# The order of the two column pieces in FFN's second product

## The chip, the cores and the metric

The kernel runs on one core of one Trainium2 chip. The metric is device time in microseconds (us): the median of several executions. One further execution is recorded by the hardware profiler, and every line of a profile or a trace below is from that one. Its engines are called PE (TensorE's matmuls), PEld (TensorE's weight loads), DVE (VectorE), ACT (ScalarE), POOL (GpSimd) and SP (SyncE).

## What is computed

A layer norm of x feeds two branches. One is attention over eight positions at a distance of two, with 32 heads of 20 columns; the other is a feed-forward network (FFN). Their product is added to x.

```python
def reference(A_x, A_wqkv, A_wo, B_w1, B_w2):      # 2048 tokens, D = 640, F = 1536
    xn = _layernorm(A_x)
    s = attention(xn, A_wqkv) @ A_wo               # 8 keys per token, 2 apart; 32 heads of 20
    h = _silu(xn @ B_w1)                           # 2048 x 1536
    g = _silu(h @ B_w2)                            # 2048 x 640: FFN's second product
    return A_x + s * g
```

## The kernel before

**Precision.** Each matrix product is made of three products. Both operands are split into a high and a low half (`th` and `tl` for the normed x and later for the attention's output, `sh` and `sl` for FFN's hidden values, and both halves of a weight block side by side in a ring of seven `w` buffers). High by high, high by low and low by high are added up in one bank of PSUM.

**Groups and stages.** The 2048 tokens are worked through in four groups of 512, each four tiles (t = 0 to 3) of 128. For each group the stages on TensorE are: the products for q, k and v (lines 737 to 739; the first quarter of the first group at line 676), from the second group on the output projection of the group before (`wo_phase`), and FFN (`ffn_phase`). The last group's projection (`wo_last`) ends the kernel.

**FFN.** F is cut into 12 blocks of 128, taken two at a time. `up(f)` makes a block of hidden values with 15 matmuls of 512 columns (lines 882 to 884) in a bank called `rot`. ScalarE's silu writes it out as `sh` (line 888) and as `sf` (line 889), and VectorE subtracts the two to get `sl` (line 890). `down((f, f + 1))`, the second product, adds both blocks' share to the output: 128 tokens by 640 columns for each of the four tiles. It first runs through both blocks' high halves, for each tile the pair of pieces with the weights' high half and then the pair with the low half; after that through both blocks' low halves, one pair a tile. That is 24 pairs of matmuls, called a run here. Six runs a group make 24 in all.

**The two pieces.** 640 columns don't fit one bank (512), so `tm_mm` issues each product as two matmuls with the same stationary tile `st`: a wide piece of CA = 384 columns (line 766) into the tile's own bank `a[t]`, and a narrow piece of CB = 256 (line 768) into one half of a bank `b[t // 2]` that two tiles share. Each matmul has a weight load (LDWEIGHTS) of its own in the instruction stream, so a pair loads the same tile twice. `wo_phase` and `wo_last` use `tm_mm` as well.

**The banks.** Six banks called `acc` go round by count (`bank()`). FFN takes all six. At the end of a group's FFN, ScalarE's silu (line 936) empties them into `gate`, the four wide banks first and then the two narrow ones; in the last group the order is wide, narrow, three wide, narrow. The next stage's products for q, k and v take the same banks in the same order, so its first matmul (line 737) writes the bank that ScalarE emptied first.

**What sets the order.** All work is entered in a list with durations and priorities, and a planner (class `Weave`) orders each engine's instructions by simulating them; TensorE's own work stays in the order in which it is entered. A whole call of `big` or `small` in `down` is one entry of TensorE, with the banks of both pieces as what it writes. The waits on semaphores are worked out afterwards from the buffers that each instruction touches.

Of the kernel before, what the change touches and what calls it, by code (L numbers as in the profile page):

```python
# [18 lines left out]
DC, FC = D // P, F // P  # L19
# [34 lines left out]
def tsl(t):  # L54
    return slice(t * P, (t + 1) * P)
# [157 lines left out]
def local_attention_silu_ffn(ctx: ExitStack, tc: tile.TileContext, x, wqkv, wo, w1, w2, out):  # L213
# [64 lines left out]
    def rot():  # L278
        i = take("rot", 2)
        return ROT[i], ("rot", i)  # L280
# [7 lines left out]
    def dve(n, fn, reads, writes, prio, lock=False):  # L288
        add("DVE", dv(n), fn, reads, writes, prio, lock)

    def act(n, fn, reads, writes, prio, table=None):
        add("ACT", ac(n), fn, reads, writes, prio, table=table)

    def pe(dur, fn, reads, writes):
        add("PE", dur, fn, reads, writes)
        clock[0] += dur
# [128 lines left out]
    def w_next(*want):  # L425

        i = used[0]
        assert units[i] == want and i < loaded[0], (units[i], want)
        used[0] += 1
        s, n = i % RING, width(want)  # L430
        return WR[s][:, :n], WR[s][:, n:2 * n], ("wh", s), ("wl", s)

    def w_done(n=1):
        for _ in range(n):
            w_load()


    def load_x(g, t, n=1, prio=None):
        dma(lambda: nc.sync.dma_start(XIN[:, t:t + n], rows(xg, g)[:, t:t + n]), [],
            [("xin", u) for u in range(t, t + n)], n * P * D * 4, clock[0] if prio is None else prio,  # L440
            late=LATE if g else 0.4 * t)

    def ln_stats(t, after=()):
        st = ST[t % 2]
        ks = ("st", t % 2)
        for k in range(2):
            dve(320, lambda k=k: nc.vector.bn_stats(out=st[:, k, :], in_=XIN[:, t, k * 320:(k + 1) * 320]),
                [("xin", t), *after], [ks + (k,)], 1)
        dve(60, lambda: nc.vector.bn_aggr(out=MV[:, t, :], in_=st), [ks + (0,), ks + (1,)], [("mv", t)], 1)

    def ln_rstd(a, b, at=1, after=()):
        n = range(a, b)
        act(b - a, lambda: nc.scalar.activation(SD[:, 0, a:b], MV[:, a:b, 1], AF.Sqrt, bias=epst, scale=1.0),
            [("mv", t) for t in n] + list(after), [("sd", t) for t in n], 0, "sqrt")
        dve(10, lambda: nc.vector.reciprocal(out=SD[:, 1, a:b], in_=SD[:, 0, a:b]),
            [("sd", t) for t in n], [("rs", t) for t in n], at)
# [53 lines left out]
    def turn_o(cs, s, ks, i, both=False):  # L510

        for k, c in enumerate(cs):
            qs = range(c * P // CQ, ((c + 1) * P - 1) // CQ + 1)
            dve(TOK, lambda k=k, c=c: nc.vector.transpose(  # L514
                out=s[:, k, :TOK].rearrange("p (j t b) -> p t j b", j=NB, t=T),
                in_=O[:, :, c * P:(c + 1) * P].rearrange("p t (j a) -> p t j a", j=NB)),
                [("o", q, t) for q in qs for t in (0, 2)], [ks[k]], 2)
        move(s, ks, cs, "ot", ["turned"], both)
        for c in cs:
            split_sb(c, moved("ot", c), i, 0 if both else 0.4)  # L520
# [233 lines left out]
    def t_keys(i, cs, ts=range(T), kinds=("th", "tl")):  # L754
        return [(k, i, c, t) for k in kinds for c in cs for t in ts]

    def tm_banks(narrow_first=False):
        b = [bank() for t in range(T // 2)] if narrow_first else None
        a = [bank() for t in range(T)]
        return a, b or [bank() for t in range(T // 2)]  # L760

    def tm_mm(banks, t, st, w, first, last, cols=(0, 1)):
        a, b = banks
        h = t % 2
        if 0 in cols:
            nc.tensor.matmul(a[t][0][:, :CA], st, w[:, :CA], start=first, stop=last)  # L766
        if 1 in cols:
            nc.tensor.matmul(b[t // 2][0][:, h * CB:(h + 1) * CB], st, w[:, CA:], start=first and h == 0,  # L768
                             stop=last, skip_group_check=True)

    def tm_views(banks, order="aaaabb"):

        a, b = banks
        n = {"a": 0, "b": 0}
        for kind in order:
            k = n[kind]
            n[kind] += 1
            if kind == "a":
                yield a[k][0][:, :CA].rearrange("p (t m) -> p t m", t=1), a[k][1], slice(k, k + 1), slice(0, CA)
            else:  # L780
                yield b[k][0].rearrange("p (t m) -> p t m", t=2), b[k][1], slice(2 * k, 2 * k + 2), slice(CA, D)

    def gkeys(ts, cs):
        return [("g", t, cs.start) for t in range(ts.start, ts.stop)]
# [84 lines left out]
    def ffn_phase(g, i, ix, io):  # L869
        nxt = g + 1 if g + 1 < NG else None  # L870
        ps = tm_banks()
        a, b = ps

        def up(f):
            wh, wl, kh, kl = w_next("w1", f)
            h, kp = rot()
            s = f % 2

            def first():
                for c in range(DC):  # L880
                    cs = tsl(c)
                    nc.tensor.matmul(h, wh[:, cs], TH[i][:, c, :], start=c == 0, stop=False)  # L882
                    nc.tensor.matmul(h, wh[:, cs], TL[i][:, c, :], start=False, stop=False)  # L883
                    nc.tensor.matmul(h, wl[:, cs], TH[i][:, c, :], start=False, stop=c == DC - 1)  # L884
            pe(15 * mm(TOK), first, t_keys(i, range(DC)) + [kh, kl], [kp])
            w_done()
            sf, sh, sl = SF[s], SH[s], SL[s]
            act(TOK, lambda: nc.scalar.activation(sh, h, AF.Silu), [kp], [("sh", s)], 0, "silu")  # L888
            act(TOK, lambda: nc.scalar.activation(sf, h, AF.Silu), [kp], [("sf", s)], 0, "silu")
            dve(TOK, lambda: nc.vector.tensor_tensor(out=sl, in0=sf, in1=sh.bitcast(F32), op=OP.subtract),  # L890
                [("sf", s), ("sh", s)], [("sl", s)], 0, lock=True)

        def down(fs):
            ws = {f: w_next("w2", f) for f in fs}
            ko = [[a[t][1], b[t // 2][1]] for t in range(T)]
            for f in fs:
                sh, ksh = SH[f % 2], ("sh", f % 2)
                wh, wl, kh, kl = ws[f]
                for t in range(T):
                    def big(t=t, f=f, sh=sh, wh=wh, wl=wl):  # L900
                        tm_mm(ps, t, sh[:, tsl(t)], wh, f == 0, False)
                        tm_mm(ps, t, sh[:, tsl(t)], wl, False, False)
                    near = f == FC - 1 and t == 0
                    pe(2 * TM, big, [ksh, kh, kl], ko[t] + ["near"] * near)
                    if near:
                        act(1, lambda: nc.scalar.activation(SD[:, 0, 0:1], epst, AF.Silu), ["near"], [("sd", 0)], 0, "silu")
            for f in fs:
                sl, ksl = SL[f % 2], ("sl", f % 2)
                wh, wl, kh, kl = ws[f]
                for t in range(T):  # L910
                    def small(t=t, f=f, sl=sl, wh=wh):
                        tm_mm(ps, t, sl[:, tsl(t)], wh, False, f == FC - 1)
                    pe(TM, small, [ksl, kh], ko[t])
                w_done()

        if nxt is None:
            for c in range(3):
                turn_o((c,), RAWS[:, c % 2:c % 2 + 1], [("raw", c % 2)], io)
            turn_o((3, 4), RAWS, [("raw", 0), ("raw", 1)], io, True)
        for f in range(0, FC, 2):  # L920
            if nxt is not None and f == X_IN:
                load_x(nxt, 0, 2)
                load_x(nxt, 2, 2)
            up(f)
            up(f + 1)
            if nxt is not None and f == X_IN:
                for t in range(T):
                    ln_stats(t)
                ln_rstd(0, T, after=[("sf", 1)])
                for t in range(T):  # L930
                    ln_apply(t)
                turn_x(g, ix)
            down((f, f + 1))
        for p, kp, ts, cs in tm_views(ps, "aaaabb" if nxt is not None else "abaaab"):
            n = (ts.stop - ts.start) * (cs.stop - cs.start)
            act(n, lambda p=p, ts=ts, cs=cs: nc.scalar.activation(G[:, ts, cs], p, AF.Silu), [kp], gkeys(ts, cs), 0.1 if nxt is None else -1, "silu")
# [42 lines left out]
```

## Time and profile before

| | |
|---|---|
| median of 3 runs | 621.68 us (621.67 to 622.61) |
| profiled execution | 621.44 us |
| its span, first to last instruction | 619.7 us |
| instructions | 9092, of which 3357 matmuls and as many weight loads |
| mean granted clock of TensorE | 0.999 |

The page's group of the wide piece with `sh` counts 384 matmuls, and so does the narrow one's; with `sl` it is 192 each. That is 24 runs of 16 and of 8. A matmul's duration in the trace is modelled and longer than its share of the engine's time, since the next one starts before it ends: the time from one start to the next is what a matmul costs.

### The profile page before, as it was taken

To read this page: it belongs to the slowest core of one execution; us is meant where nothing else is said; L and a number is where in the kernel's file an instruction comes from. 1 tells how busy PE (TensorE), PEld (TensorE's weight loads), DVE (VectorE), ACT (ScalarE), POOL (GpSimd) and SP (SyncE) were. 2 spreads that over 40 slices of the span, in tenths; PEclk is the share of its full clock that TensorE was granted. 3 is DMA by queue.
4 is the path that set the end of the run, shared out by engine and by line. 5 is a ranking of instruction groups with operands and counts; after the bars stand their busy time and mean duration, and the time that the engine had idled before them with its cause. 6 is when DMAs were issued, how large, how long until landed. Compare 5 with 4: busy or idle time off the path is not lost.

```text
span 619.7 us, 9092 instructions
## 1 busy us (share of the span) xinstructions
PE 614.2 (99%) x3357; PEld 555.3 (90%) x3357; DVE 561.3 (91%) x581; ACT 309.5 (50%) x651; POOL 112.8 (18%) x168
## 2 busy tenths in 40 slices
PE   8999999999999999999999999999999999999997
PEld 7889999998889999999888999999888999998997
DVE  6558999999989997999998999999979999899974
ACT  5435558937376213951944502583396316152750
POOL 4510000011101133111212233311121213311100
PEclk9999999999999999999999999999999999999999
DMA  8999999866999998764699999855579998956642
GB/s 248 343 287 324 354 345 391 356 236 186 304 322 348 328 356 259 238 195 139 203 242 251 340 333 304 276 176 163 169 202 278 251 334 277 316 179 202 206 124 103
DMA packets 65449, 162.45 MB, mean 262 GB/s; under 512 B 7053, under 2 KB 29165, under 8 KB 65405
## 3 DMA queue, kind: packets, MB, share of 16 engines
q0 software_dynamic: 20016, 82.58, 44.6%
q1 hardware_dynamic: 45389, 79.29, 40.6%
q8 instruction: 26, 0.43, 0.3%
q14 instruction: 18, 0.15, 0.1%
HBM read 109.55 MB, written 34.16 MB: 232 GB/s over the span
## 4 chain that ended last, share of the span: by engine, by line
PE 98%; SPq 1%; DMA 0%; DVE 0%; issue 0%
PE acc L766 22%; PE acc L768 15%; PE acc L737 10%; PE acc L739 10%; PE acc L738 10%; PE rot L883 9%; PE rot L884 9%; PE rot L882 9%; PE acc L676 2%; PE rot L768 1%; DMA pr<-in_A_wqkv_dram 0%; PE rot L766 0%; SPq L376 0%; PE acc L864 0%; SPq L377 0%; PE rot L654 0%
## 5 line engine op out<-in xcount | busy, mean ns | idle before, releaser
L739 PE MATMUL acc<-w,th 128*128 128x512 f32 (+1 forms) x300 | 112.4, 375 | 0.0
L738 PE MATMUL acc<-w,tl 128*128 128x512 f32 (+1 forms) x300 | 112.4, 375 | 0.0
L737 PE MATMUL acc<-w,th 128*128 128x512 f32 (+1 forms) x300 | 112.4, 375 | 0.0
L766 PE MATMUL acc<-w,sh 128*128 128x384 f32 x384 | 111.7, 334 | 0.0
L768 PE MATMUL acc<-w,sh 128*128 128x256 f32 x384 | 107.1, 279 | 0.0
L888 ACT ACTIVATE sh<-rot 128x512 fp32r<-128x512 f32 x48 | 28.6, 597 | 154.2 <-PE rot L884 154.2
L884 PE MATMUL rot<-th,w 128*128 128x512 f32 x240 | 93.8, 391 | 0.0
L883 PE MATMUL rot<-tl,w 128*128 128x512 f32 x240 | 93.8, 391 | 0.0
L882 PE MATMUL rot<-th,w 128*128 128x512 f32 x240 | 93.5, 389 | 0.0
L571 DVE TENSOR_TENSOR pr<-q,kv 128x2560 f32<-128x2560 f32 x32 | 90.2, 2819 | 1.2 <-DMA raw<-in_A_wqkv_dram 1.0
L609 DVE TENSOR_TENSOR pr<-e,kv 128x2560 f32<-128x2560 f32 x32 | 90.3, 2823 | 0.7
L574 DVE TENSOR_REDUCE l<-pr 128x128 f32<-128x2560 f32 x32 | 90.1, 2815 | 0.5
L614 DVE TENSOR_TENSOR pr<-pr 128x1280 f32<-128x1280 f32 x64 | 74.0, 1156 | 1.5
L402 POOL DMA_DIRECT2D w<-half_w x72 | 38.5, 534 | 190.1 <-PE acc L768 94.0
L766 PEld LDWEIGHTS acc<-w,sh 128*128 128x128 f32 x384 | 72.1, 188 | 1.1
L768 PEld LDWEIGHTS acc<-w,sh 128*128 128x128 f32 x384 | 72.2, 188 | 0.9
L402 POOL DMA_DIRECT2D w<-half_q x52 | 27.6, 531 | 238.8 <-PE rot L884 113.5
L737 PEld LDWEIGHTS acc<-w,th 128*128 128x128 f32 x300 | 56.3, 188 | 8.6
L739 PEld LDWEIGHTS acc<-w,th 128*128 128x128 f32 x300 | 56.3, 188 | 8.6
L738 PEld LDWEIGHTS acc<-w,tl 128*128 128x128 f32 x300 | 56.3, 188 | 8.6
L487 ACT ACTIVATE xin<-sf 32x256 f32<-32x256 f32 (+1 forms) x144 | 54.6, 379 | 9.7 <-DVE sf L514 8.0
L766 PE MATMUL acc<-w,sl 128*128 128x384 f32 x192 | 56.1, 332 | 0.0
(104 smaller groups left out, 1059.5 us busy)
## 6 DMA issues: line engine op xcount, KB each, us to landing
w<-half_w POOLq DMA_DIRECT2D x72, 640.0 KB, 6.1
w<-half_q POOLq DMA_DIRECT2D x39, 512.0 KB, 4.3
half_w<-w SPq DMA_DIRECT2D x24, 640.0 KB
w<-half_wo POOLq DMA_DIRECT2D x15, 640.0 KB, 5.6
kv<-kv SPq DMA_DIRECT2D x15, 560.0 KB
half_q<-w SPq DMA_DIRECT2D x15, 512.0 KB
kv<-kv SPq DMA_DIRECT2D x15, 420.0 KB
gate<-in_B_w_dram SPq DMA_DIRECT2D x16, 320.0 KB
```

The lines of the kernel that those rows point to most:

```text
L571: dve(2560, lambda t=t: nc.vector.tensor_tensor(out=PR, in0=win(qq[:, t:t + 2, :], W, 0), in1=win(kv[:, 0, t:t + 2, :], W, CQ), op=OP.mult ...
L574: dve(2560, lambda t=t: nc.vector.tensor_reduce(out=l[:, t:t + 2].rearrange("p t w h -> p (t w h)"), in_=PR.rearrange("p t w (h d) -> p (t ...
L609: dve(2560, lambda t=t, v=v: nc.vector.tensor_tensor(out=PR.rearrange("p t w (h d) -> p t (w h) d", d=DH), in0=e[:, t:t + 2].rearrange("p ...
L614: dve(2 * k * CQ, lambda k=k: nc.vector.tensor_tensor(out=PR[:, :, 0:k, :], in0=PR[:, :, 0:k, :], in1=PR[:, :, k:2 * k, :], op=OP.add), [] ...
L737: nc.tensor.matmul(o, hi, wh, start=c == 0, stop=False)
L738: nc.tensor.matmul(o, lo, wh, start=False, stop=False)
L739: nc.tensor.matmul(o, hi, wl, start=False, stop=c == DC - 1)
L766: nc.tensor.matmul(a[t][0][:, :CA], st, w[:, :CA], start=first, stop=last)
L768: nc.tensor.matmul(b[t // 2][0][:, h * CB:(h + 1) * CB], st, w[:, CA:], start=first and h == 0, stop=last, skip_group_check=True)
L882: nc.tensor.matmul(h, wh[:, cs], TH[i][:, c, :], start=c == 0, stop=False)
L883: nc.tensor.matmul(h, wh[:, cs], TL[i][:, c, :], start=False, stop=False)
L884: nc.tensor.matmul(h, wl[:, cs], TH[i][:, c, :], start=False, stop=c == DC - 1)
```

## The change

In the pairs of FFN's second product the narrow piece is issued ahead of the wide one. `tm_mm` now follows the order given in `cols`, and the three calls in `down` pass (1, 0). The projection's calls keep their order, (0, 1), or a single piece.

```diff
     def tm_mm(banks, t, st, w, first, last, cols=(0, 1)):
         a, b = banks
         h = t % 2
-        if 0 in cols:
+        def wide():
             nc.tensor.matmul(a[t][0][:, :CA], st, w[:, :CA], start=first, stop=last)
-        if 1 in cols:
+
+        def narrow():
             nc.tensor.matmul(b[t // 2][0][:, h * CB:(h + 1) * CB], st, w[:, CA:], start=first and h == 0,
                              stop=last, skip_group_check=True)
+        for k in cols:
+            (wide, narrow)[k]()
...
                     def big(t=t, f=f, sh=sh, wh=wh, wl=wl):
-                        tm_mm(ps, t, sh[:, tsl(t)], wh, f == 0, False)
-                        tm_mm(ps, t, sh[:, tsl(t)], wl, False, False)
+                        tm_mm(ps, t, sh[:, tsl(t)], wh, f == 0, False, (1, 0))
+                        tm_mm(ps, t, sh[:, tsl(t)], wl, False, False, (1, 0))
...
                     def small(t=t, f=f, sl=sl, wh=wh):
-                        tm_mm(ps, t, sl[:, tsl(t)], wh, False, f == FC - 1)
+                        tm_mm(ps, t, sl[:, tsl(t)], wh, False, f == FC - 1, (1, 0))
```

In the changed kernel the narrow piece is line 769, and every later line is 3 higher (line 936 becomes 939).

TensorE, the start of the first run of the first group, before: the last 512-column matmuls of `up`, then the pairs of tile 0 and the first piece of tile 1. `acc_111` and `acc_112` are the wide banks of tiles 0 and 1, `acc_109` the narrow bank of both; in brackets is the engine whose semaphore an instruction waits for.

```order
L884 MATMUL rot_114<-th_69,w_73 128x512
L766 MATMUL acc_111<-w_74,sh_81 128x384 [waits Activation_49]
L768 MATMUL acc_109<-w_74,sh_81 128x256
L766 MATMUL acc_111<-w_74,sh_81 128x384 [waits DVE_49]
L768 MATMUL acc_109<-w_74,sh_81 128x256
L766 MATMUL acc_112<-w_74,sh_81 128x384
```

The same place in the changed kernel:

```order
L887 MATMUL rot_114<-th_69,w_73 128x512
L769 MATMUL acc_109<-w_74,sh_81 128x256 [waits Activation_49]
L766 MATMUL acc_111<-w_74,sh_81 128x384
L769 MATMUL acc_109<-w_74,sh_81 128x256 [waits DVE_49]
L766 MATMUL acc_111<-w_74,sh_81 128x384
L769 MATMUL acc_109<-w_74,sh_81 128x256
```

The waits for `sh` (Activation) and for the weights' low half (DVE) stay at the first and the third matmul of the run and are now on narrow pieces.

TensorE, the end of the first group's last run and the start of the next stage, before. `acc_107` and `acc_108` are the wide banks of tiles 2 and 3, `acc_110` their narrow bank; L737 begins the next group's products in `acc_111`, tile 0's wide bank.

```order
L766 MATMUL acc_107<-w_74,sl_84 128x384
L768 MATMUL acc_110<-w_74,sl_84 128x256
L766 MATMUL acc_108<-w_74,sl_84 128x384
L768 MATMUL acc_110<-w_74,sl_84 128x256
L737 MATMUL acc_111<-w_75,th_70 128x512 [waits DMASW0_49,Activation_49]
```

And in the changed kernel:

```order
L769 MATMUL acc_110<-w_74,sl_84 128x256
L766 MATMUL acc_107<-w_74,sl_84 128x384
L769 MATMUL acc_110<-w_74,sl_84 128x256
L766 MATMUL acc_108<-w_74,sl_84 128x384
L737 MATMUL acc_111<-w_75,th_70 128x512 [waits DMASW0_49,Activation_49]
```

The run now ends with a wide piece, and L737 keeps its wait for ScalarE's emptying of `acc_111`.

ScalarE, the emptying of the six banks behind that run, before:

```order
L936 ACTIVATE gate<-acc_111 128x384 [waits PE_49]
L936 ACTIVATE gate<-acc_112 128x384 [waits PE_49]
L936 ACTIVATE gate<-acc_107 128x384 [waits PE_49]
L936 ACTIVATE gate<-acc_108 128x384 [waits PE_49]
L936 ACTIVATE gate<-acc_109 128x2x256
L936 ACTIVATE gate<-acc_110 128x2x256 [waits PE_49]
```

And in the changed kernel:

```order
L939 ACTIVATE gate<-acc_111 128x384 [waits DVE_49,PE_49]
L939 ACTIVATE gate<-acc_112 128x384 [waits PE_49]
L939 ACTIVATE gate<-acc_107 128x384 [waits PE_49]
L939 ACTIVATE gate<-acc_108 128x384 [waits PE_49]
L939 ACTIVATE gate<-acc_109 128x2x256
L939 ACTIVATE gate<-acc_110 128x2x256
```

The last narrow bank has no wait of its own any more, and in this group the first emptying also names VectorE. Nothing else moves: on the other engines the instructions stand in the same order as before.

## The prediction

> **What bounds the kernel now.** I read the page's first parts, then the table of who waited for whom on TensorE, then the timeline at the places the change touches.
>
> ```profile
> PE 614.2 (99%) x3357; PEld 555.3 (90%) x3357; DVE 561.3 (91%) x581; ACT 309.5 (50%) x651; POOL 112.8 (18%) x168
> PEclk9999999999999999999999999999999999999999
> PE 98%; SPq 1%; DMA 0%; DVE 0%; issue 0%
> PE acc L766 22%; PE acc L768 15%; PE acc L737 10%; PE acc L739 10%; PE acc L738 10%; PE rot L883 9%; PE rot L884 9%; PE rot L882 9%; PE acc L676 2%; PE rot L768 1%; DMA pr<-in_A_wqkv_dram 0%; PE rot L766 0%; SPq L376 0%; PE acc L864 0%; SPq L377 0%; PE rot L654 0%
> ```
>
> TensorE is busy for 99% of the span at full granted clock and makes up 98% of the chain that ended last. The two lines with the largest shares of that chain, L766 (384 columns) and L768 (256 columns), are the ones whose order changes. A busy matmul row proves little, since matmuls overlap, so the waits come next:
>
> ```profile
> engine line waited for: us in total, times, longest us
> PE rot L627 <- POOL ident masks.py:199: 1.4, 1, 1.4
> PE acc L676 <- DMA pr<-in_A_wqkv_dram: 0.3, 1, 0.3
> ```
>
> That is the whole table for TensorE: two waits, both in the first stage, none in FFN. So the time moves only if the change alters how fast the pieces follow each other, or creates a wait where there is none. Here is the start of one run of the second product, then its end (columns: start in us, modelled duration, what ran).
>
> ```profile
> 68.60 0.34 PE L766 MATMUL acc<-w,sh 128*128 128x384 f32 x1
> 68.78 0.28 PE L768 MATMUL acc<-w,sh 128*128 128x256 f32 x1
> 68.90 0.34 PE L766 MATMUL acc<-w,sh 128*128 128x384 f32 x1
> 69.07 0.28 PE L768 MATMUL acc<-w,sh 128*128 128x256 f32 x1
> 69.19 0.34 PE L766 MATMUL acc<-w,sh 128*128 128x384 f32 x1
> ...
> 69.76 0.33 PE L766 MATMUL acc<-w,sh 128*128 128x384 f32 x1
> ...
> 70.91 0.33 PE L766 MATMUL acc<-w,sh 128*128 128x384 f32 x1
> ...
> 73.20 0.33 PE L766 MATMUL acc<-w,sl 128*128 128x384 f32 x1
> ...
> 75.38 0.28 PE L768 MATMUL acc<-w,sl 128*128 128x256 f32 x1
> 75.50 0.40 PE L882 MATMUL rot<-th,w 128*128 128x512 f32 x1
> ```
>
> The modelled durations (0.34, 0.28) overlap; what counts is from start to start. A wide piece holds TensorE for about 0.17 us (68.90 to 69.07), a narrow one for 0.12 (69.07 to 69.19), and a run of 24 pairs takes 75.50 − 68.60 = 6.90 us, 287.5 ns a pair. There are 24 such runs (12 blocks of F, two at a time, in four groups), 576 pairs, some 166 us of the span.
>
> **The change, part by part.**
>
> *The pieces themselves.* Nothing is added or removed: 576 wide and 576 narrow pieces, each with its own weight load, before and after. Each hands over after its own time, so the sum of a run is the same in either order: **0**. It depends on one thing, that this time belongs to the piece and not to its neighbour. Three places could break that.
>
> *The weight load at a change of token tile.* Both pieces of a pair load the same stationary tile; a new one comes at the first piece of a tile. Before, that load runs beneath a narrow piece; now it runs beneath a wide one, and the narrow piece covers only a repeated load. If a new tile cost more than a repeat, this would gain. From 70.91 to 73.20 there are eight pairs and four new tiles (2.29 us); from 73.20 to 75.50 eight pairs and eight new tiles (2.30). Four more new tiles cost at most the rounding, 0.01 us, or 2.5 ns each. There are 384 new tiles in all, so the bound is 1.0 us, either sign. I take 0, since 68.78 to 68.90 (the same tile) and 69.07 to 69.19 (a new one) are both 0.12. The Trainium skill, "TensorE: Matmul & The Clock Gate", section "LDWEIGHTS (loading the stationary operand)", puts a load at columns ÷ 1.2 ns, an estimated 107 ns for 128 columns, which would just fit beneath either piece; by it the term is 0 as well, and it speaks against the gain below. The trace agrees where a late load is seen by itself: the rows of 263.47 and 263.58, quoted next, are two loads 0.11 us apart.
>
> *Waits that move to the other piece.* The first piece of a run waits for `sh` or `sl`, the third for the low half of the weights, whichever piece it is. One such wait is late in the profiled execution:
>
> ```profile
> 262.82 0.60 ACT L888 ACTIVATE sh<-rot 128x512 fp32r<-128x512 f32 x1
> ...
> 263.32 0.28 PE L768 MATMUL acc<-w,sh 128*128 128x256 f32 x1
> 263.47 0.19 PEld L766 LDWEIGHTS acc<-w,sh 128*128 128x128 f32 x1
> ...
> 263.58 0.19 PEld L768 LDWEIGHTS acc<-w,sh 128*128 128x128 f32 x1
> ```
>
> ScalarE finished `sh` at 263.42, the load followed 0.05 later, at 263.47, and TensorE lost some 0.15 us (a load normally starts with the piece ahead of it, here 263.32). The run's later `sh` comes at the same moment in the new order, and a load must start about 0.12 ahead of its matmul in either order. So the 0.15 stays, cost of the move **0**; nothing gets earlier or later behind it, because the run's total is the same. The release of a weight slot, for which GpSimd's issues wait (L402), now hangs on a wide piece that starts 0.05 earlier and drains 0.05 longer: also 0.
>
> *The hand-over of the banks at the end of a group.* This is the one place where something becomes later. In the last run of groups 0 to 2 the wide bank of tile 0 is finished behind its narrow piece, 0.12 us later than before. ScalarE's first L936 empties it, and the next stage's first L737 writes it again.
>
> ```profile
> 143.42 0.49 ACT L936 ACTIVATE gate<-acc 128x384 f32<-128x384 f32 x1 [4.74 <-PE acc L766]
> 144.08 0.19 PEld L737 LDWEIGHTS acc<-w,th 128*128 128x128 f32 x1
> 144.19 0.40 PE L737 MATMUL acc<-w,th 128*128 128x512 f32 x1
> ...
> 144.90 0.39 PE L737 MATMUL acc<-w,th 128*128 128x512 f32 x1
> ...
> 294.93 0.49 ACT L936 ACTIVATE gate<-acc 128x384 f32<-128x384 f32 x1 [4.80 <-PE acc L766]
> 295.53 0.19 PEld L737 LDWEIGHTS acc<-w,th 128*128 128x128 f32 x1
> ...
> 446.24 0.49 ACT L936 ACTIVATE gate<-acc 128x384 f32<-128x384 f32 x1 [2.13 <-PE acc L766]
> 446.84 0.19 PEld L737 LDWEIGHTS acc<-w,th 128*128 128x128 f32 x1
> ```
>
> ScalarE was idle and released by L766 itself, so L936 moves by the full 0.12. The load of L737 may then start at 143.42 + 0.49 + 0.12 + 0.05 = 144.08, 295.59 and 446.90, against 144.08, 295.53 and 446.84 now. That is late by 0.00, 0.06 and 0.06: **+0.12 us**. Bounds: 0, if the 0.05 is shorter here, and 3 × 0.12 = 0.36, if no slack is left. The next tile's L737 comes 0.7 us later (144.90 beside 144.19, three 512-column pieces) while ScalarE needs at most another 0.49 for its bank, so only the first is late. Group 3 has no such hand-over of its wide bank: ScalarE reaches it later, behind copies that it runs until 598.62:
>
> ```profile
> 596.50 2.12 ACT L487 ACTIVATE xin<-raw 32x256 f32<-32x256 f32 x5
> 598.65 0.49 ACT L936 ACTIVATE gate<-acc 128x384 f32<-128x384 f32 x1
> ```
>
> *The seams with the 512-column pieces.* A run now begins 512 to 256 and ends 384 to 512. The trace has the second seam once, where the first FFN stage follows L739:
>
> ```profile
> 61.59 0.33 PE L739 MATMUL acc<-w,th 128*128 128x384 f32 x1
> 61.76 0.39 PE L882 MATMUL rot<-th,w 128*128 128x512 f32 x1
> ...
> 82.34 0.34 PE L766 MATMUL acc<-w,sh 128*128 128x384 f32 x1
> ```
>
> Those 30 pieces took 61.76 to 68.60, 6.84 us; the next 30, behind a narrow piece, 75.50 to 82.34, 6.84 as well. At 0.01 us a run, 24 runs bound this at ±0.24; I take 0. For the first seam there is no row; the first four pairs of a run take 69.76 − 68.60 = 1.16 us where four settled ones take 1.15, so the start costs 0.01 now. Losing or doubling that is ±0.24 again; I take 0.
>
> **The sum.** The profiled execution took 621.44 us, 619.7 of it span and 1.74 around it. 621.44 + 0.12 = 621.56. It lies 0.24 below the median of the three runs, inside what repeats differ by (621.67 to 622.61). I predict **621.6**.
>
> **The rivals.**
>
> *The settled pace is lost (slower).* A pair is not equally fast everywhere. The same pairs in the output projection, with `th` as the stationary tile:
>
> ```profile
> 195.47 0.33 PE L766 MATMUL acc<-w,th 128*128 128x384 f32 x1
> ...
> 213.06 0.40 PE L882 MATMUL rot<-th,w 128*128 128x512 f32 x1
> ```
>
> 60 pairs in 17.59 us, 293.2 ns each, with no wait: 5.7 ns slower than in FFN's second product. And a run of that begins at this slower pace too (68.60 to 68.90 is 0.30, 68.90 to 69.19 is 0.29) before it settles. If starting with the narrow piece kept it from settling, 576 × 5.7 ns = 3.3 us would come on top: **624.8**. It counts as slower from 1.24 us, 2.2 ns a pair. For it: the reason for the two paces isn't in the trace. Against: once settled a run stays so across new tiles, new weights and both kinds of `s`, through the same alternation that the change keeps.
>
> *The new tile's load was the tight one (faster).* The full bound of 1.0 us and both seams' 0.48 together: 621.44 − 1.48, about **620.0**. For it speaks only that the trace's rounding allows it; equal gaps of 0.12 speak against it.
>
> *A later bank wait (slower).* The last narrow bank has no wait of its own any more; it is covered by that of the last wide bank. If the first L936 were likewise released only by the last matmul of the run, it would start near 144.35 (the run's last matmul, 0.12 ahead of 144.19 and 0.28 long, as the one at 75.38 ahead of 75.50) instead of 143.42, its bank would be free 0.93 later, 0.8 beyond the slack, three times: 2.4 us, **623.9**. Against: all four wide banks keep a wait of their own.
>
> *The change doesn't take effect.* Then 621.4, the same verdict; the order of instructions excludes it.
>
> **Chances.** The forecast 0.87, the lost pace 0.07, the faster case 0.03, the later wait 0.03. A measurement of this kernel can tell about 0.2% (1.24 us) from no change; faster by more: 0.04 (the faster case and a little of the forecast's edge), slower by more: 0.10, within: 0.86. The range is the forecast with its largest unknown, ±1.0 for the tile loads, and with the highest repeat: 620.5 to 622.7.
>
> **What would show it.** In the changed profile the pair should still take 287 to 288 ns over a run of 6.90 us (a wrong first step shows as 293). A new row for L737 behind L936, of some 0.06 us, twice, may appear among TensorE's waits; none, or three of 0.9, would refute that step. The runs of 512-column pieces should keep 6.84 us. I'd be wrong by more than the range only if the pace of a pair depends on which piece comes first.

## The result and the profile after

The changed kernel took **627.53 us** (median of 4 runs, 627.41 to 630.16) against 621.67 before (621.31 to 622.61 in 4 runs). The ratio on record, which is not the quotient of the two medians, is 1.0105, with a 95% interval from 1.0089 to 1.0121: slower by about 1%, and outside the predicted 620.5 to 622.7.

From the changed kernel's page: busy time by engine, the clock row, the chain that ended last by engine, and the groups of the two pieces with `sh` (total busy time, then the mean modelled duration of one, in ns).

```profile
PE 620.2 (99%) x3357; PEld 561.6 (90%) x3357; DVE 562.0 (90%) x581; ACT 309.7 (50%) x651; POOL 112.9 (18%) x168
PEclk9999999999999999999999999999999999999999
PE 99%; DVE 0%; ACT 0%; issue 0%; POOL 0%; POOLq 0%
L766 PE MATMUL acc<-w,sh 128*128 128x384 f32 x384 | 115.7, 342 | 0.0
L769 PE MATMUL acc<-w,sh 128*128 128x256 f32 x384 | 108.3, 282 | 0.0
```

TensorE still fills the span at full clock, and its table of waits still names none in FFN. What changed is the pieces themselves: a wide one now shows 342 ns where it showed 334, a narrow one 282 where it showed 279. The table of TensorE's waits in the changed kernel:

```profile
engine line waited for: us in total, times, longest us
PE rot L627 <- POOL ident masks.py:199: 1.4, 1, 1.4
PE acc L676 <- ACT w L410: 0.3, 1, 0.3
```

The same shows in the timeline (start, modelled duration). First two settled pairs and both ends of the second run in the changed kernel:

```profile
82.42 0.28 PE L769 MATMUL acc<-w,sh 128*128 128x256 f32 x1
...
83.30 0.28 PE L769 MATMUL acc<-w,sh 128*128 128x256 f32 x1
83.42 0.34 PE L766 MATMUL acc<-w,sh 128*128 128x384 f32 x1
83.60 0.28 PE L769 MATMUL acc<-w,sh 128*128 128x256 f32 x1
...
83.90 0.28 PE L769 MATMUL acc<-w,sh 128*128 128x256 f32 x1
...
89.60 0.39 PE L885 MATMUL rot<-th,w 128*128 128x512 f32 x1
```

and the same run before, which started at 82.34:

```profile
83.22 0.33 PE L766 MATMUL acc<-w,sh 128*128 128x384 f32 x1
83.39 0.28 PE L768 MATMUL acc<-w,sh 128*128 128x256 f32 x1
83.50 0.33 PE L766 MATMUL acc<-w,sh 128*128 128x384 f32 x1
...
83.79 0.33 PE L766 MATMUL acc<-w,sh 128*128 128x384 f32 x1
...
89.24 0.40 PE L882 MATMUL rot<-th,w 128*128 128x512 f32 x1
```

A wide piece now holds TensorE for 0.18 us (83.42 to 83.60) in place of 0.17, and a settled pair takes 0.30 us (83.30 to 83.60 to 83.90) in place of 0.285 (83.22 to 83.79 is two). The run takes 89.60 − 82.42 = 7.18 us against 6.90. Here is where the 6.0 us of span (625.7 − 619.7) come from: 24 runs × 0.28 = 6.7 more. A run of 512-column pieces behind a wide piece is 0.02 shorter, and there are some twenty of those, 0.4 less:

```profile
75.60 0.39 PE L885 MATMUL rot<-th,w 128*128 128x512 f32 x1
```

(75.60 to 82.42 is 6.82; before, 75.50 to 82.34 was 6.84.) And the first run happened to begin at 68.28 us where it began at 68.60, 0.3 less. The projection's pairs, which the change doesn't touch, keep their pace.

### The profile page after: what moved, and what is told of

Its sections match the earlier page's. It is cut to its first block, busy times and chain, and to the rows that moved or that the text cites. A ratio compares the mean times of both kernels' runs of the same rounds, so it can differ in the third digit from the quotient of the medians.

```text
span 625.7 us, 9094 instructions
## 1 busy us (share of the span) xinstructions
PE 620.2 (99%) x3357; PEld 561.6 (90%) x3357; DVE 562.0 (90%) x581; ACT 309.7 (50%) x651; POOL 112.9 (18%) x168
## 4 chain that ended last, share of the span: by engine, by line
PE 99%; DVE 0%; ACT 0%; issue 0%; POOL 0%; POOLq 0%
PE acc L766 23%; PE acc L769 15%; PE acc L739 10%; PE acc L737 10%; PE acc L738 10%; PE rot L886 9%; PE rot L885 9%; PE rot L887 9%; PE acc L676 2%; PE rot L627 1%; PE rot L769 1%; PE rot L766 0%; PE rot L654 0%; PE acc L867 0%; ACT w L410 0%
## 5 line engine op out<-in xcount | busy, mean ns | idle before, releaser
L766 PE MATMUL acc<-w,sh 128*128 128x384 f32 x384 | 115.7, 342 | 0.0
L737 PE MATMUL acc<-w,th 128*128 128x512 f32 (+1 forms) x300 | 112.4, 375 | 0.0
L737 PEld LDWEIGHTS acc<-w,th 128*128 128x128 f32 x300 | 56.3, 188 | 8.6
L766 PE MATMUL acc<-w,sl 128*128 128x384 f32 x192 | 58.6, 342 | 0.0
```

What stands on the lines that cost most here:

```text
L737: nc.tensor.matmul(o, hi, wh, start=c == 0, stop=False)
```

## The experiments

**What was in question.** The same 48 matmuls a run, in another order, take 4% longer, with no wait. Four theories were set against each other. *A*: the pace hangs on where the stationary tile lies in SBUF relative to the moving operand, together with the order. *B*: the way in which a run begins sets a pace that then lasts. *C*: the weights' columns are now read backwards (384 to 639, then 0 to 383), and that costs. *D*: the load of a new tile beneath a wide piece costs.

The changed kernel's own trace already speaks against D: in the low halves every pair brings a new tile, in the high halves every second one, and both run at 0.30.

A came from the code. `sh` and `sl` don't follow the weight ring directly. A tile of 48 bytes, `st1`, is allocated between them, so that they lie 64 bytes further on than whole tiles would put them. In the built program the ring begins at byte 58112 of a partition and `sh` at 94016; `th`, the projection's stationary tile, at 17152. Modulo 512 these are 256, 320 and 256: `sh` stands 64 bytes from the ring, `th` 0.

All kernels below but two were executed once, so their times carry the spread of single executions; the kernel before, executed once beside them, took 621.22 to 621.46 us. The verdicts go by the length of a run, read from each trace at its second run. Within one trace the runs agree to 0.02 us, but for the first and the tenth, which in many traces have a wait in them.

### Where sh lies, at 0 bytes

```diff
     WR = tiles("w", RING, [P, 2 * D], F32R)
-    ST.append(sb.tile([P, 2, 6], F32, name="st1"))
     SH = tiles("sh", 2, [P, TOK], F32R)
     SL = tiles("sl", 2, [P, TOK], F32R)
+    ST.append(sb.tile([P, 2, 6], F32, name="st1"))
```

Expected of the changed kernel with this edit:

> Changed kernel (narrow piece first), with the small tile st1 allocated behind sl in place of between the weight ring and sh: sh and sl lie 64 bytes lower, nothing else moves. Theory A (the pace of a pair hangs on the offset between the stationary tile's address and the moving operand's, together with the order): the offset becomes that of the projection's th, so the pair takes the projection's 293 ns, a run 7.04 us, the kernel about 624.5 us. Theory B (how a run is entered sets its pace), C (going back in w's columns costs) and D (a new tile's load beneath the wide piece costs): nothing changes, 300 ns, 7.18 us a run, 627.5 us.

and of the kernel before with it:

> Kernel before (wide piece first) with the same move of st1. A: the advantage of the 64 bytes goes, 293 ns a pair, 7.04 us a run, the kernel some 3 us slower, 624.5 us. B, C, D: 287 ns, 6.90 us a run, 621.5 us.

Measured: 627.17 and 623.59 us. The ends of the second run, narrow first and then wide first:

```profile
85.06 0.28 PE L769 MATMUL acc<-w,sh 128*128 128x256 f32 x1
...
92.10 0.39 PE L885 MATMUL rot<-th,w 128*128 128x512 f32 x1
```

```profile
82.12 0.33 PE L766 MATMUL acc<-w,sh 128*128 128x384 f32 x1
...
89.16 0.39 PE L882 MATMUL rot<-th,w 128*128 128x512 f32 x1
```

7.04 us in both. Without the 64 bytes FFN's pairs run at the projection's pace, and **the order makes no difference**. A stands; B, C and D had said 7.18 and 6.90. That the narrow-first kernel's time was nevertheless 627.17 is mostly due to two waits of that execution in the first group, from its table of waits for weight loads:

```profile
PEld acc L769 <- DVE sl L893: 1.6, 1, 1.6
...
PEld acc L737 <- ACT q L528: 1.2, 1, 1.2
```

Such waits of 1 to 2 us stand in traces of both orders, and they come and go: of two traces of one wide-first kernel (128 bytes, below), one has its first run at 8.47 us and the other at 6.92. The timed pair below shows the spread.

### The direction of the columns

```diff
-            nc.tensor.matmul(a[t][0][:, :CA], st, w[:, :CA], start=first, stop=last)
+            nc.tensor.matmul(a[t][0][:, :CA], st, w[:, CB:], start=first, stop=last)
...
-            nc.tensor.matmul(b[t // 2][0][:, h * CB:(h + 1) * CB], st, w[:, CA:], start=first and h == 0,
+            nc.tensor.matmul(b[t // 2][0][:, h * CB:(h + 1) * CB], st, w[:, :CB], start=first and h == 0,
```

with the output's columns moved along in all that reads the banks.

> Changed kernel, but in all calls the narrow piece takes columns 0 to 255 of the weights and the wide one 256 to 639; FFN issues the narrow one first, so that w's columns are read upwards; the projections keep wide first and now read downwards. C: FFN's pairs go back to about 287 ns, 6.90 us a run, and the projection's rise above 293. A, B, D: FFN stays at 300 ns, 7.18 us a run, 627.5 us, the projection at 293.

Measured: 629.94 us; 7.17 us for the second run (84.91 to 92.08), and the projection's three stages 17.59 us each as before. **C falls.**

### How a run begins

```diff
-                        tm_mm(ps, t, sh[:, tsl(t)], wh, f == 0, False)
+                        tm_mm(ps, t, sh[:, tsl(t)], wh, f == 0, False, (1, 0) if f == fs[0] and t == 0 else (0, 1))
```

This is an edit of the kernel before, with `tm_mm` following `cols` as in the change; all other pairs stay wide first.

> Narrow first in the first pair of each run only, wide first in the 23 others. B: the run keeps the pace with which it was entered, 300 ns a pair, 7.18 us. A, C, D: 287 ns from the second pair on, 6.90 to 6.92 us a run, 621.5 us.

The counterpart has (0, 1) there, and all other pairs narrow first:

> Wide first in the first pair of each run only, narrow first in the 23 others (the counterpart of e4_first_pair), at the 64-byte offset. If the entry picks one of two lasting paces, whichever piece comes first: 287 ns from about the fourth pair on, 6.88 to 6.92 us a run, 621.5 us, although 23 of 24 pairs are narrow first. If the two adjacent pieces of one width behind the odd pair are what led to the slow pace in e4: 300 ns, 7.15 to 7.18 us a run, 627.5 us. If it was the narrow piece somewhere in the run that did it: also 300 ns.

Measured: 628.48 and 627.33 us. The ends of the second run, the first with one narrow-first pair of 24, the second with one wide-first pair of 24:

```profile
84.16 0.28 PE L769 MATMUL acc<-w,sh 128*128 128x256 f32 x1
...
91.32 0.40 PE L885 MATMUL rot<-th,w 128*128 128x512 f32 x1
```

```profile
82.54 0.34 PE L766 MATMUL acc<-w,sh 128*128 128x384 f32 x1
...
89.70 0.39 PE L885 MATMUL rot<-th,w 128*128 128x512 f32 x1
```

7.16 us each. The first is decisive: 23 pairs stand exactly as in the kernel before, and they settle at 300 ns. So **the pace isn't a property of a pair's order; it lasts from the beginning of the run on**, as long as no wait interrupts the run, and B holds at this layout. Not every beginning with a wide piece leads to the fast pace, as the second shows. A is not contradicted: at 0 bytes both orders led to one and the same pace.

The same odd pair in the middle (`f == fs[1] and t == 0`, pair 9 of 24):

> Kernel before (64 bytes, wide first) with one pair of each run turned round, the first pair of the second block, a third of the way through (pair 9 of 24). If the pace is a lasting state that a disturbance can switch: 287 ns a pair up to there and 300 behind it, although 15 of the 16 pairs from there on are wide first; some 7.07 us a run, 625.5 us. If the entry from the 512-column pieces alone sets it: 287 throughout, 6.90 us, 621.5 us. If the pace belongs to the order of each pair by itself: one pair of 300 and 23 of 287, 6.91 us.

Measured: 621.52 us. The beginning, the odd pair's narrow piece ahead of its wide ones, and the end:

```profile
82.25 0.34 PE L766 MATMUL acc<-w,sh 128*128 128x384 f32 x1
...
84.44 0.39 PE L769 MATMUL acc<-w,sh 128*128 128x256 f32 x2
84.67 0.51 PE L766 MATMUL acc<-w,sh 128*128 128x384 f32 x2
85.02 0.28 PE L769 MATMUL acc<-w,sh 128*128 128x256 f32 x1
...
89.15 0.40 PE L885 MATMUL rot<-th,w 128*128 128x512 f32 x1
```

6.90 us: the fast pace, once there, survives the odd pair, which itself costs nothing. The reading that an odd pair anywhere switches the pace falls.

### What stands ahead of a run

The last 512-column matmul of each `up` is split in two, so that a run is entered behind a piece of 256 columns; pairs and addresses stay.

```diff
-                    nc.tensor.matmul(h, wl[:, cs], TH[i][:, c, :], start=False, stop=c == DC - 1)
+                    for half in ((slice(0, TOK),) if c < DC - 1 else (slice(0, 256), slice(256, TOK))):
+                        nc.tensor.matmul(h[:, half], wl[:, cs], TH[i][:, c, half], start=False, stop=half.stop == TOK and c == DC - 1)
```

In the changed kernel, and in the kernel before:

> Changed kernel (narrow first), the last 512-column matmul of each up split in two of 256 columns (48 matmuls more, each with a weight load); the pairs are untouched, but a run is entered behind a 256-column piece. The split itself costs some 48 x 0.01 us = 0.5 us. If the entry picks the pace: either pace is possible, 6.90 or 7.18 us a run, and 6.90 would show that the narrow piece in front is not what makes it slow; 7.18 leaves it open.

> Kernel before (wide first, 64 bytes, nothing moved), the last 512-column matmul of each up split in two of 256 columns, as in e11_split_entry. The pairs and all addresses are those of before; only what stands ahead of a run differs. If the entry picks the pace: 7.16 to 7.18 us a run is possible, and would show it with no pair touched, about 628 us; if wide first at these addresses leads to the fast pace from any entry: 6.88 to 6.92 us, 622 us.

Measured: 630.06 and 624.06 us; the second run 7.18 us (84.14 to 91.32) and 6.88 (84.39 to 91.27). Each keeps its pace. So the width of what went before doesn't pick it.

The run's own first pieces alone don't pick it either, as the first run of the narrow-first trace shows. Its first weight load had to wait for `sh`, and its first low half waited for `sl`:

```profile
68.52 0.19 PEld L769 LDWEIGHTS acc<-w,sh 128*128 128x128 f32 x1 [0.20 <-ACT sh L892]
68.74 0.33 PE L766 MATMUL acc<-w,sh 128*128 128x384 f32 x1
...
73.04 0.33 PE L766 MATMUL acc<-w,sh 128*128 128x384 f32 x1
74.78 0.38 PE L769 MATMUL acc<-w,sl 128*128 128x256 f32 x1 [1.41 <-DVE sl L894]
75.00 0.34 PE L766 MATMUL acc<-w,sl 128*128 128x384 f32 x1
...
77.10 0.34 PE L766 MATMUL acc<-w,sl 128*128 128x384 f32 x1
```

From 68.74 to 73.04 there are 15 pairs, 287 ns each: plain narrow first, in the order and layout of the second run and its 7.18 us, at the fast pace behind a late start. Behind the second wait the seven pairs from 75.00 to 77.10 take 300. Waits inside a run switched the pace in other traces too: in the kernel with the odd first pair the tenth run went from 300 to 287 behind a late `sh` and took 7.03 us in place of 7.16. Not every wait does it: the kernel before kept 287 behind the wait in its tenth run. So a pace lasts until a wait interrupts the stream, and may be picked anew there; that the exact moment of the start picks it would suit this, but no experiment varied that moment alone.

### Other places for sh, wide first

```diff
     ST.append(sb.tile([P, 2, 6], F32, name="st1"))
+    sb.tile([P, 16], F32, name="gap16")
```

This makes 128 bytes; 32 columns make 192; 8 columns without `st1` make 32.

> Kernel before (wide first) with 64 bytes more between the weight ring and sh: the offset of sh and sl from the ring is 128 bytes. If what counts is whether the offset is a multiple of 128 bytes: 293 ns as without an offset, 7.04 us a run, 623.6 us. If any offset that is not a multiple of 512 does: 287 ns or 300 ns, 6.90 or 7.18 us a run.

> Kernel before (wide first) with 32 bytes between the weight ring and sh. If an offset shifts the meeting of the two reads by its length, a pace between the known ones or a new one, not 287 or 293; if only whole 64-byte steps count, 293 ns (7.04 us a run, 623.6 us) or 287 ns (6.90 us, 621.5 us).

> Kernel before (wide first), sh 192 bytes from the weight ring. If the offset counts modulo 128 bytes: as with 64, 6.90 us a run (or 7.18 in the other state), 621.5 us. Otherwise another pace; the offsets seen so far gave 7.04 (0), 7.03 (32), 6.89 (64) and 6.92 us (128), so modulo 128 is already unlikely.

Measured: 622.37, 624.36 and 625.14 us; the second run 6.92 us at 128 bytes, 7.03 at 32 and 7.03 at 192. Only 64 and 128 leave the common 7.03 to 7.04; neither "modulo 128" nor "any offset" is the rule.

### The change at 128 bytes

> Changed kernel (narrow first) with 64 bytes more between the weight ring and sh, so 128 in all; the wide-first kernel of this layout ran at 6.92 us a run. If the slow pace belongs to the narrow piece leading: 7.15 us a run or more, 627 us or more. If it is one of two paces that the 64-byte layout allows, and this layout has one: 6.90 to 6.94 us a run whichever piece leads, 622 us, and the change costs nothing here.

Measured: 623.14 us, with the ends of the second run

```profile
84.00 0.29 PE L770 MATMUL acc<-w,sh 128*128 128x256 f32 x1
...
90.91 0.40 PE L886 MATMUL rot<-th,w 128*128 128x512 f32 x1
```

6.91 us, the fast pace with the narrow piece first. Both orders of this layout were then timed:

> The kernel of e6_gap128 again (wide first, sh 128 bytes from the weight ring), timed: 6.92 us a run, 622.0 to 622.6 us.

> The kernel of e9_gap128_narrow again (narrow first, 128 bytes), timed. If the change costs nothing where the layout has one pace, and the single wait of 1.78 us in the first group of that one look is not the order's doing: within 0.2% of e14_gap128_wide_timed, 621.2 to 622.6 us. If the narrow piece in front brings that wait about: 623 us or more in most runs.

Measured against the kernel before (621.45 us, 620.98 to 623.38 in 19 runs): wide first 622.48 us (622.13 to 625.10 in 10 runs), ratio 1.0022 (1.0008 to 1.0036); narrow first 622.90 us (621.07 to 624.44 in 10 runs), ratio 1.0008 (0.9991 to 1.0026). The two intervals overlap: at this layout **no cost of the change can be told from noise**. The narrow-first median lies outside what I had set, with runs near 621.1 and others near 624. The profiled one, 623.68 us, has a wait of the first group in it:

```profile
PEld acc L770 <- DVE sl L894: 1.5, 1, 1.5
```

Is this layout free of the slow pace, then? The odd first pair, at 128 bytes:

> The kernel of e4_first_pair (first pair of each run turned round) with sh 128 bytes from the weight ring. If this layout has one pace only: 287 ns, 6.90 to 6.94 us a run, 622.5 us, where e4 took 7.16. If one odd pair slows any layout: 7.1 us or more.

Measured: 628.84 us, and the second run

```profile
82.79 0.29 PE L770 MATMUL acc<-w,sh 128*128 128x256 f32 x1
...
89.98 0.40 PE L886 MATMUL rot<-th,w 128*128 128x512 f32 x1
```

7.19 us, so the reading of one pace for this layout falls: it has two as well. It only happens that both plain orders usually begin in the way that leads to the fast one.

### The ring moved by 64 and by 128 bytes

```diff
+    sb.tile([P, 16], F32, name="gap16")
     WR = tiles("w", RING, [P, 2 * D], F32R)
```

`sh` stays 64 bytes from the ring, but ring and `sh` lie 64 bytes further on, and `th` and `tl` now have 64 bytes to the ring as well. Wide first, then narrow first:

> Kernel before with 64 bytes put ahead of the weight ring: sh keeps its 64 bytes from the ring, and th and tl, until now at a multiple of 512 bytes from it, get 64 as well. If the offset alone makes the paces: FFN's second product stays at 287 ns, and the projection's pairs leave 293 ns for 287 or 300 (-1.2 or +1.2 us over its 180 pairs and the same for wo_last), with some change in the stages of 512 columns too. If th's tiles are slower for another reason, all stays: 621.5 us.

> Changed kernel (narrow first) with 64 bytes ahead of the weight ring; in this layout the wide-first kernel took the slow pace, 7.20 us a run, 633.1 us. If the pace is a matter of the moment at which a run is entered and not of which piece leads: the narrow-first kernel may well take the fast one here, 6.90 us a run and some 626.5 us; the order would then work the other way round. If the narrow piece in front is slow at any 64-byte offset: 7.18 to 7.20 us, 633 us.

Measured: 633.14 and 626.29 us. The second runs:

```profile
82.90 0.34 PE L767 MATMUL acc<-w,sh 128*128 128x384 f32 x1
...
90.10 0.40 PE L883 MATMUL rot<-th,w 128*128 128x512 f32 x1
```

```profile
82.86 0.28 PE L770 MATMUL acc<-w,sh 128*128 128x256 f32 x1
...
89.75 0.39 PE L886 MATMUL rot<-th,w 128*128 128x512 f32 x1
```

7.20 us wide first, 6.89 narrow first. **Here the change makes the kernel faster by about 1%** (one execution of each), by the same 0.3 us a run by which it made the original slower. Neither beats the kernel before, since the 512-column pieces are slower in this layout (see the last section). The projection's pairs kept 17.59 to 17.60 us, 293 ns a pair, in both, although `th` and `tl` stood 64 bytes from the ring: they lie below it, `sh` above. So a distance of 64 bytes doesn't by itself give the paces of 287 and 300; whether it matters which of the two lies lower, no run shows.

With 128 bytes ahead of the ring, wide first:

> Kernel before with 128 bytes ahead of the weight ring: sh stays 64 bytes from it, at the same places modulo 128 as before, while th and tl get 128 from the ring. If the offset makes the paces and 128 does for th what it does for sh: the projection's pairs go from 293 to 287 ns, 1.2 us less there and some 0.3 in wo_last; FFN's second product keeps 287, or takes 300 if its entry from the 512-column pieces has changed. If 512-column pieces gain too (272 cycles for 256 of streaming): several us less. Else 621.5 us.

Measured: 629.90 us; the second run 6.88 us (82.97 to 89.85), but the projection 18.00 us (197.83 to 215.83) for its 60 pairs, 300 ns each where it had 293, and the 512-column pieces slower as well. No gain lies there.

## Why the prediction was wrong

**What bounds the kernel** was right: TensorE's own stream, with 0.2 us or less lost to waits in FFN before and after. So was its first conclusion, that time can only move with the pace of the pieces or a new wait.

**The step that failed** is the first of the sum, "*The pieces themselves*", costed at 0 on one condition: that the time a piece holds TensorE "belongs to the piece and not to its neighbour". It doesn't. With `sh` 64 bytes from the ring a stream of pairs has two lasting paces, 287 and 300 ns, and the way it starts picks one: plain wide first starts into the fast one, plain narrow first into the slow one, unless a wait comes between. The experiments show both orders at both paces (wide first at 300 behind an odd first pair and with the ring moved; narrow first at 287 with the ring moved, at 128 bytes, and at the original places behind a late start), and the same pace for both orders at 0 bytes. What failed in the argument was taking a gap measured in one settled stream for a constant of the piece, although the profile before had two paces for the same pair (287.5 and 293.2) and gave no reason for it.

**The rival named this mechanism and mispriced it.** "*The settled pace is lost*" had 0.07 and 624.8 us, since the projection's 293 ns was the slowest pair in sight. The runs showed that 293 is the pace of another layout, not this one's upper end: 300 makes 24 × 0.28 = 6.7 us. The bound taken from the nearest rows was no bound, because no row of the trace showed the other state. The argument against it, that a settled run stays settled across new tiles and weights, was true where no wait interrupts the run (it even survives an odd pair in its middle) and beside the point: the question was how it begins, and the quoted rows of 68.60 to 69.19 showed that beginning to be a phase of its own.

**The weight load at a change of token tile**, 0: right. Runs with a new tile in every pair and in every second one keep the same 0.30.

**Waits that move to the other piece**, 0: right in sum, not in detail. The late `sh` costs the tenth run 0.04 us now (7.22 against 7.18) where it cost 0.15 (7.04 against 6.89), and the first run has a new delay of 0.14 (7.32) where its low halves begin; TensorE's table of waits names neither.

**The hand-over of the banks**, +0.12: too large. In the changed kernel, at the second of these places (TensorE's loads and matmuls there):

```profile
298.32 0.34 PE L766 MATMUL acc<-w,sl 128*128 128x384 f32 x1
298.40 0.19 PEld L737 LDWEIGHTS acc<-w,th 128*128 128x128 f32 x1
298.50 0.41 PE L737 MATMUL acc<-w,th 128*128 128x512 f32 x1
298.74 0.40 PE L738 MATMUL acc<-w,tl 128*128 128x512 f32 x1
```

The load of L737 starts late, 0.08 behind the start of the piece ahead of it; 0.06 had been computed. But it now lies beneath a wide piece, which holds TensorE for 0.18, so L737 still starts on time (298.32 + 0.18). At most 0.01 is lost, where the next piece follows after 0.24 in place of the 0.23 that it took before (295.65 to 295.88). I had kept the old cover of 0.12 for the load.

**The seams**, 0 within ±0.24 each: 512-column runs behind a wide piece became 0.02 shorter, 0.4 us in all, a little beyond that bound. The beginning of a run I had bounded by losing or doubling its 0.01; that it decides over the pairs behind it was not in the sum.

**Still open.** What at a start picks the pace, and what the two paces are physically. That the reads of the stationary tile and of the moving operand get in each other's way, depending on where they lie and at which moment they meet, would suit all of this, but it was only argued; shown are the dependence on the placement and on the way a run begins, and that a wait can change the pace.

## What to carry to other kernels

On a stream of matmuls without waits, the time from start to start need not be a constant of the shape; here it wasn't. Look whether the same shape has different paces in different stages of the trace, and if so, count an unexplained pace as something that any reordering may gain or lose, for the whole stream. Try a reordering at two or three placements of the operands (here a pad of 64 bytes ahead of a tile was enough) before calling one order better. And price a rival by what an unseen state could cost, not by the slowest row in sight.

## What the runs showed of the hardware

A pad of 64 bytes, with no instruction changed, moved this kernel by up to 1.9% (633.14 us with it ahead of the ring, 621.46 for the kernel before, executed beside it, once each). The slow pair pace makes 24 × 0.3 = 7.2 of these 11.7 us. The rest is mostly in the 512-column matmuls, whose stationary tile is now in the moved ring and whose moving operand is `th`; with the ring moved by 64 and by 128 bytes:

```profile
90.10 0.40 PE L883 MATMUL rot<-th,w 128*128 128x512 f32 x1
...
97.10 0.34 PE L767 MATMUL acc<-w,sh 128*128 128x384 f32 x1
```

```profile
89.85 0.39 PE L883 MATMUL rot<-th,w 128*128 128x512 f32 x1
...
96.82 0.33 PE L767 MATMUL acc<-w,sh 128*128 128x384 f32 x1
```

30 pieces take 7.00 and 6.97 us, 233 and 232 ns each, where they took 6.84, 228. The pace of a settled pair took one of three values, 287, 293 and 300 ns, 6 to 7 ns apart, to within 1 ns, in every layout and order tried.
